# Retention and two MLPs on one core: where the first chunk's increments, weight conversions and warm-up matmuls stand

## The chip, the core and the metric

The kernel runs on one core of a Trainium2 chip. Its time is the device time of one execution in microseconds (us). The core has a matrix engine (PE, with its weight loads shown as PEld), a vector engine (DVE), a scalar engine (ACT), GpSimd (POOL) and SyncE (SP); the last two only issue DMAs here, SP the loads and POOL the stores. Each engine takes its instructions in the order in which they stand. PE writes its results to PSUM, from which DVE and ACT read them.

## What is computed

The reference runs a decaying linear attention ("retention") over 768 tokens for 4 batches and 8 heads of 64, and sends the result, as a matrix of 3072 tokens by 512, through two MLPs with 2048 hidden units.

```
state = gamma * state + k_t (x) v_t          # per batch and head, 64 x 64
y_t   = scale * q_t @ state
x = y reshaped to 3072 x 512
x = leaky(x @ w_in) @ w_out                  # leaky(h) = max(0.01 h, h)
out = relu(x @ w2_in)**2 @ w2_out
```

The weights come as 64-bit numbers whose words are float64 bit patterns; the kernel turns them into float32 itself, and then splits each float32 matrix into a high and a low part, so that a product is three matmuls (high by high, low by high, high by low).

## The kernel before

The tokens are worked in chunks of 256 (`C`), and a pair `(u, p)` is one batch's chunk for two heads (`p` of `NP` = 4). The first chunk has 16 pairs, numbered here 0 to 15 in the order of `ups`, and they are what the program does first, with the first weights being loaded and converted beside them. In the first chunk a pair's work is dealt over two turns of the start loop (`for n in range(n0 + 1)`):

- `scores(pair n)`: four score matmuls into the tile `sc` (two PSUM banks, tag `sc`, two buffers) and two matmuls of `increment`, the sum of k (x) v over the pair's first 128 tokens, into columns 256 to 319 of the first of these banks. DVE multiplies the scores by the decay mask (`pm`, line 220), and ACT copies the increment to SBUF (`s1`, line 235), which is the state after 128 tokens.
- `values(pair n-1)`: matmuls into a bank `y` of the pool `ps_h` (three banks, tag `h`): state times q, the second increment, masked scores times v. Then ACT casts y to `xh` (line 272), DVE makes the new `state` (line 278) and the low part `xl` (line 282), and the bank is free.
- `prep_pair` scales q (DVE, line 179) and v (ACT, line 189) for a pair that comes two turns later.

Between these stand the steps of `first_in(q)`, a generator that converts the input weights of hidden tiles 0 and 1 (`in_steps`): ACT scales the high words (`high`) and the low words (`low`), DVE shifts, puts in the sign and adds, and `up` splits the result into `wa`. One step is taken per turn from turn 6 on, two from turn 14. `emit_plain(q, i, t)` is a projection of 512 tokens by 128 hidden units: 12 matmuls into a bank `pa` of `ps_h`, then an Lrelu on ACT (line 741), then for t = 0 the split into `gh` (ACT, 762) and `gl` (DVE, 763). It stands after turn 14 for hidden tile 0, and for tile 1 after the loop.

`make_out(q)` converts the output weights of hidden tiles 2q and 2q+1: `cast` (ACT lines 382, 383; DVE lines 384, 385, 388) and then `pair_up` into `wo` (ACT line 414, DVE line 415). `put_out` (through `emit_out`) multiplies by `wo` into the banks `acc`; its first call comes after the projection `emit_plain(1, 0, 0)`.

The order on each engine is the order of emission where an instruction goes through `pin` (all matmuls and DMAs, and everything in `seq` while `strict[0]` is set). What is not pinned is placed by a scheduler. `aside()` holds it back: its instructions are issued after the two marked instructions (`mark`), which are here the last projection's Lrelu. `load_w(q, half)` puts the load of a raw weight tile `sg` (two buffers) on SP's queue; half 0 is the input part, half 1 the output part. A load waits in SP's queue until its buffer is free, and the loads behind it wait with it.

The start of the program makes `busy(WARM)` matmuls on zeros into the bank `idle`.

Of the kernel before, what the change touches and what calls it, by code (L numbers as in the profile page):

```python
# [9 lines left out]
F32 = mybir.dt.float32  # L10
# [3 lines left out]
AF = mybir.ActivationFunctionType  # L14
ALU = mybir.AluOpType

B, H, S, D = 4, 8, 768, 64
P = 128
C = 256
# [6 lines left out]
T = 512  # L26
# [3 lines left out]
NJ = DFF // P  # L30
NQ = NJ // 2
FW = 1024
WARM = 6

# [17 lines left out]
def retention_then_two_mlps(  # L54
# [9 lines left out]
    nc = tc.nc  # L64
# [7 lines left out]
    ps_h = ctx.enter_context(tc.tile_pool(name="ps_h", bufs=3, space=bass.MemoryType.PSUM))  # L72
# [30 lines left out]
    @contextmanager  # L103
    def aside():

        with tc.issue_after(mark[0]), tc.issue_after(mark[1]):
            yield
# [14 lines left out]
    def seq(ins):  # L122

        return pin(ins) if strict[0] else ins
# [9 lines left out]

    ups = [(b, p) for t in range(2) for p in range(NP) for b in (2 * t, 2 * t + 1)]
    ups += [(c * B + b, p) for c in range(1, NC) for p in range(NP) for b in range(B)]
    raw, prep, sc_ps, ps = {}, {}, {}, {}
    xs = {}


# [60 lines left out]
    def scores(up, alone):  # L201
        u, p = up
        c, b = divmod(u, B)
        raw_qk = raw[up][0]
        if u < B:
            sc2 = ps["s"].tile([P, 2, 512], F32, tag="sc", name="sc")
            sc = [sc2[:, h] for h in range(2)]
        else:
            other = (ps["a"], "y") if alone else (ps_h, "h")
            sc = [p.tile([P, 512], F32, tag=t, name="sc") for p, t in ((ps_h, "h"), other)]  # L210
        for s in range(2):
            t = slice(s * P, s * P + P)
            for h in range(2):
                a = slice(64 * h, 64 * h + 64)
                mm(out=sc[h][:, t], lhsT=raw_qk[a, C + t.start:C + t.stop], rhs=raw_qk[a, t], start=True, stop=True)
        sp = sc[0][:, C:C + D]
        increment(up, 0, sp)
        if u < B:
            both = prep[up][2]
            seq(nc.vector.tensor_tensor(  # L220
                out=both.rearrange("p h (s t) -> p h s t", t=P),
                in0=sc2[:, :, 0:C].rearrange("p h (s t) -> p h s t", t=P),
                in1=mk[p].unsqueeze(2).to_broadcast([P, 2, 2, P]), op=ALU.mult,
            ))
            pm = [both[:, h] for h in range(2)]
        else:
            pm = [a_p.tile([P, C], F32, tag="pm", name="pm") for h in range(2)]
            for h in range(2):
                nc.vector.tensor_tensor(
                    out=pm[h].rearrange("p (s t) -> p s t", t=P), in0=sc[h][:, 0:C].rearrange("p (s t) -> p s t", t=P),  # L230
                    in1=mk[p][:, h].unsqueeze(1).to_broadcast([P, 2, P]), op=ALU.mult,
                )
        s1 = a_p.tile([P, D], F32, tag="s1", name="s1", bufs=3)
        if c == 0:
            seq(nc.scalar.copy(s1, sp))
        else:
            nc.vector.scalar_tensor_tensor(
                out=s1, in0=state[:, b, p], scalar=gt[p], in1=sp, op0=ALU.mult, op1=ALU.add,
            )
        sc_ps[up] = pm, s1  # L240

    def values(up):
        u, p = up
        c, b = divmod(u, B)
        vk = raw[up][1]
        qs = prep[up][0]
        pm, s1 = sc_ps.pop(up)
        y = (ps["a"] if c else ps_h).tile([P, T], F32, tag="y" if c else "h", name="y")
        for s in range(0 if c else 1, 2):
            st = s1 if s else state[:, b, p]  # L250
            for h in range(2):
                a = slice(64 * h, 64 * h + 64)
                mm(
                    out=y[a, s * P:s * P + P], lhsT=st[a], rhs=qs[a, s],
                    start=s == 0 or not c, stop=False, skip_group_check=True,
                )
        if c < NC - 1:
            increment(up, 1, y[:, C:C + D], False)
        for s in range(2):
            for h in (1, 0):  # L260
                mm(
                    out=y[64 * h:64 * h + 64, s * P:s * P + P], lhsT=vk[:, s * P + h * D:s * P + h * D + D],
                    rhs=pm[h][:, s * P:s * P + P], start=False, stop=True, skip_group_check=True,
                )
        if c == 0:

            t, kh = b // 2, p // 2
            if (t, kh) not in xop:
                i = ((1, 5), (6, 3))[t][kh]
                xop[t, kh] = [x_p.tile([P, 2, T], F32R, tag=f"x{l}{i}", name=f"x{l}{i}") for l in "hl"]  # L270
            hi, lo = (x[:, p % 2, b % 2 * C:b % 2 * C + C] for x in xop[t, kh])
            seq(nc.scalar.copy(hi, y[:, 0:C]))
        else:
            if c not in xs:
                xs[c] = x_p.tile([P, KB, TB], F32, tag="xs", name="xs")
            nc.scalar.copy(xs[c][:, p, b * C:b * C + C], y[:, 0:C])
        if c < NC - 1:
            seq(nc.vector.scalar_tensor_tensor(
                out=state[:, b, p], in0=s1, scalar=gt[p], in1=y[:, C:C + D], op0=ALU.mult, op1=ALU.add,
            ))  # L280
        if c == 0:
            seq(nc.vector.tensor_tensor(out=lo, in0=y[:, 0:C], in1=hi.bitcast(F32), op=ALU.subtract))
        prep.pop(up)
        raw.pop(up)
# [53 lines left out]
    def load_w(q, half):  # L338
        if q == NQ:
            return  # L340
        t = stage[q, half] = w_p.tile([P, 1024], U64, tag="sg", name="sg", bufs=2)
        load(out=t, in_=w1[q, half])
# [74 lines left out]
    def in_steps(s, f, to):  # L417

        word = s.bitcast(U32).rearrange("p (n t) -> p n t", t=2)
        h = [slice(0, 512), slice(512, 1024)]  # L420
        lo, hi = word[:, :, 0], word[:, :, 1]
        ru = f.bitcast(U32)

        def high(c):
            seq(nc.scalar.activation(out=f[:, c], in_=hi.bitcast(F32)[:, c], func=AF.Copy, scale=2.0 ** -112))
            seq(nc.vector.tensor_scalar(
                out=ru[:, c], in0=ru[:, c], scalar1=3, scalar2=None, op0=ALU.logical_shift_left,
            ))

        def low(c):  # L430
            seq(nc.scalar.activation(out=lo[:, c], in_=lo[:, c], func=AF.Copy, scale=2.0 ** -29))

        def sign(c):
            seq(nc.vector.scalar_tensor_tensor(
                out=ru[:, c], in0=hi[:, c], scalar=0x80000000, in1=ru[:, c], op0=ALU.bitwise_and, op1=ALU.bitwise_or,
            ))

        def add(c):
            seq(nc.vector.tensor_tensor(out=ru[:, c], in0=ru[:, c], in1=lo[:, c], op=ALU.add))

        def up(n):
            t, r = to[:, :, 2 * n:2 * n + 2], f[:, h[n]].rearrange("p (n c) -> p n c", n=2)
            seq(nc.scalar.copy(t[:, 0], r))
            seq(nc.vector.tensor_tensor(out=t[:, 1], in0=r, in1=t[:, 0].bitcast(F32), op=ALU.subtract))

        high(h[0])
        yield
        low(h[0])
        sign(h[0])
        yield  # L450
        high(h[1])
        add(h[0])
        yield
        low(h[1])
        sign(h[1])
        yield
        add(h[1])
        yield
        up(0)
        yield  # L460
        up(1)
# [95 lines left out]
    def make_out(q):  # L557
        if q < NQ - 1:
            f = g_p.tile([P, 2, T], F32, tag=f"t{NQ - 1}", name="of", bufs=1).rearrange("p j c -> p (j c)")
        else:  # L560
            f = w_p.tile([P, 1024], F32, tag="wf", name="of", bufs=1)
        cast(stage.pop((q, 1)), f, 1 if q else 2)
        o = o_p.tile([P, 4, 2, 256], F32R, tag="wo", name="wo", bufs=2)
        pair_up(o.rearrange("p n l c -> p l n c"), f.rearrange("p (n c) -> p n c", n=4))
        put_wou(q, o)
# [430 lines left out]

    busy(WARM)
    n0 = B * NP
# [7 lines left out]
    for n in range(n0 + 1):  # L1006
        if n == 0:
            load_w(0, 0)
        loads_to(min(n + 6, n0))
        if n == 11:  # L1010
            loads_to(n0 + 2)
        if n in (6, 12):
            load_w(2 - n // 6, n // 12)
        score_next(n0)
        if n < 3:
            busy(2 - n // 2)
        if n in (6, 14):
            steps = first_in(n // 14)
        for _ in range(1 + (n > 13) if n < n0 else 0):
            next(steps, None)  # L1020
        value_to(min(n, n0))
        prep_to(min(n + (2 if n < 2 else 3), n0 + 2))
        if n == 14:
            emit_plain(0, 0, 0)
# [2 lines left out]
    load_w(1, 1)  # L1027
    emit_plain(0, 1, 0)
    strict[0] = False
    make_out(0)  # L1030
    start.close()
    ps["acc"] = ctx.enter_context(tc.tile_pool(name="ps_acc", bufs=1, space=bass.MemoryType.PSUM))
    ps["a"] = early.enter_context(tc.tile_pool(name="ps_a", bufs=1, space=bass.MemoryType.PSUM))
# [246 lines left out]
```

## Time and profile before

| | us |
|---|---|
| median of 3 runs | 1122.57 |
| lowest and highest of them | 1118.81, 1127.09 |
| profiled execution, its time | 1124.68 |
| profiled execution, its span | 1122.9 |

| engine | busy us | share of the span |
|---|---|---|
| PE | 1099.7 | 98% |
| DVE | 704.4 | 63% |
| ACT | 582.1 | 52% |

The span runs from the first to the last instruction of the profiled execution; its time holds 1.8 us around that. A busy share of an engine counts what the profile shows as running, at whatever clock. The chain of waits is the work that ended last, followed back from the end of the program.

### The profile page before, as it was taken

To read this page: it belongs to the slowest core of one execution; us is meant where nothing else is said; L and a number is where in the kernel's file an instruction comes from. 1 tells how busy PE (TensorE), PEld (TensorE's weight loads), DVE (VectorE), ACT (ScalarE), POOL (GpSimd) and SP (SyncE) were. 2 spreads that over 40 slices of the span, in tenths; PEclk is the share of its full clock that TensorE was granted. 3 is DMA by queue.
4 is the path that set the end of the run, shared out by engine and by line. 5 is a ranking of instruction groups with operands and counts; after the bars stand their busy time and mean duration, and the time that the engine had idled before them with its cause. 6 is when DMAs were issued, how large, how long until landed. Compare 5 with 4: busy or idle time off the path is not lost.

```text
span 1122.9 us, 15253 instructions
## 1 busy us (share of the span) xinstructions
PE 1099.7 (98%) x5643; PEld 872.4 (78%) x5643; DVE 704.4 (63%) x1205; ACT 582.1 (52%) x1052; POOL 78.0 (7%) x134
## 2 busy tenths in 40 slices
PE   9799999899999999999999999999999999999998
PEld 6477777678777776788788788788888888888886
DVE  4576766755657555526557738885745777555853
ACT  4466665534646453335555446655455555455542
POOL 0000100101000010001111021200100000000000
PEclk9899999999999999999999999999999999999999
DMA  9368887766598876588895877988245866357571
GB/s 366 131 240 312 326 285 233 280 198 228 208 351 299 335 264 222 190 313 322 327 316 197 321 275 271 354 325 317 112 169 197 327 206 262 112 191 249 180 243 57
DMA packets 81227, 283.87 MB, mean 253 GB/s; under 512 B 7808, under 2 KB 10368, under 8 KB 72960
## 3 DMA queue, kind: packets, MB, share of 16 engines
q1 hardware_dynamic: 64208, 210.33, 54.2%
q0 software_dynamic: 16800, 72.36, 16.5%
q8 instruction: 45, 0.74, 0.3%
q10 hardware_dynamic: 144, 0.20, 0.1%
q14 instruction: 30, 0.25, 0.1%
HBM read 205.79 MB, written 77.07 MB: 252 GB/s over the span
## 4 chain that ended last, share of the span: by engine, by line
PE 77%; issue 7%; DMA 7%; DVE 5%; ACT 2%; POOL 1%; SPq 0%; POOLq 0%; ACTq 0%; DVEq 0%
PE acc L127 38%; PE pa L127 21%; PE pd L127 7%; PE y L127 4%; PE pb L127 3%; DMA r<-first 3%; PE sc L127 3%; DMA sg<-w 2%; DMA wo<-wou 1%; POOL wou L133 1%; DMA of<-wflt 1%; PE idle L127 1%; DVE pm L220 0%; DMA wf<-wraw 0%; DVE of L385 0%
## 5 line engine op out<-in xcount | busy, mean ns | idle before, releaser
L127 PE MATMUL acc<-rot,wu 128*128 128x512 f32 x1008 | 235.7, 395 | 0.0
L127 PEld LDWEIGHTS acc<-rot,wu 128*128 128x128 f32 x1008 | 189.2, 188 | 46.0
L127 PE MATMUL pa<-xh,wa 128*128 128x512 f32 x576 | 181.2, 396 | 0.0
L127 PE MATMUL acc<-gh,wo 128*128 128x512 f32 x600 | 160.3, 399 | 3.4 <-DMA wo<-wou 2.5
L127 PEld LDWEIGHTS acc<-gh,wo 128*128 128x128 f32 x600 | 112.3, 189 | 31.6 <-issue 4.7
L127 PEld LDWEIGHTS pa<-xh,wa 128*128 128x128 f32 x576 | 106.3, 188 | 25.5 <-issue 2.2
L127 PE MATMUL pa<-xl,wa 128*128 128x512 f32 x288 | 112.6, 391 | 0.0
L837 ACT CAST rot<-gu 128x512 fp32r<-128x512 f32 x120 | 74.5, 621 | 61.5 <-PE acc L127 54.1
L838 DVE TENSOR_TENSOR rot<-gu,rot 128x512 fp32r<-128x512 f32 x120 | 82.1, 689 | 38.0 <-ACT rot L837 37.5
L127 PE MATMUL pa<-xh,wb 128*128 128x512 f32 x320 | 99.9, 393 | 0.8 <-DVE gt L863 0.8
L127 PE MATMUL pd<-xh,wa 128*128 128x512 f32 x320 | 99.1, 390 | 1.0 <-DVE wa L485 0.6
L127 PE MATMUL acc<-gl,wo 128*128 128x512 f32 x300 | 85.3, 391 | 0.0
L763 DVE TENSOR_TENSOR gl<-g,gh 128x512 fp32r<-128x512 f32 x75 | 50.6, 688 | 36.9 <-ACT gh L762 20.6
L127 PEld LDWEIGHTS pd<-xh,wa 128*128 128x128 f32 x320 | 60.0, 188 | 14.8 <-DVE wa L485 1.0
L127 PEld LDWEIGHTS pa<-xh,wb 128*128 128x128 f32 x320 | 59.4, 188 | 14.1 <-DVE gt L863 1.2
L127 PEld LDWEIGHTS acc<-gl,wo 128*128 128x128 f32 x300 | 56.5, 188 | 12.6
L127 PEld LDWEIGHTS pa<-xl,wa 128*128 128x128 f32 x288 | 54.1, 188 | 11.6
L127 PE MATMUL acc<-gg,wo 128*128 128x512 f32 x252 | 62.9, 398 | 0.0
L127 PE MATMUL pa<-xl,wb 128*128 128x512 f32 x160 | 62.4, 390 | 0.0
L127 PE MATMUL pd<-xl,wa 128*128 128x512 f32 x160 | 62.4, 390 | 0.0
L127 PEld LDWEIGHTS acc<-gg,wo 128*128 128x128 f32 x252 | 46.8, 188 | 11.9 <-issue 1.4
L687 ACT ACTIVATE gt<-gt 128x512 f32<-128x512 f32 x48 | 30.4, 633 | 48.4 <-DVE gt L856 34.3
(143 smaller groups left out, 1636.5 us busy)
## 6 DMA issues: line engine op xcount, KB each, us to landing
wu<-wou SPq DMA_DIRECT2D x84, 512.0 KB, 5.9
wo<-wou SPq DMA_DIRECT2D x32, 1024.0 KB, 7.9
wa<-wid SPq DMA_DIRECT2D x28, 1024.0 KB, 7.5
wb<-wid SPq DMA_DIRECT2D x28, 768.0 KB, 6.5
sg<-w SPq DMA_DIRECT2D x16, 1024.0 KB, 6.5
wou<-of POOLq DMA_DIRECT2D x32, 512.0 KB, 5.3
r<-first SPq DMA_DIRECT2D x50, 256.0 KB, 6.6
wid<-wa POOLq DMA_DIRECT2D x12, 1024.0 KB, 6.9
```

The costliest lines, as they stand in the source:

```text
L127: pin(nc.tensor.matmul(**kw))
L133: pin(nc.gpsimd.dma_start(**io))
L687: nc.scalar.activation(out=g, in_=g, func=AF.Relu)
L763: mark[1] = seq(nc.vector.tensor_tensor(out=gl, in0=g, in1=gh.bitcast(F32), op=ALU.subtract)).ins
L837: mark[0] = nc.scalar.copy(r[:, 0], s).ins
L838: mark[1] = nc.vector.tensor_tensor(out=r[:, 1], in0=s, in1=r[:, 0].bitcast(F32), op=ALU.subtract).ins
```

## The change

Four things, all in the start of the program:

- `WARM` goes from 6 to 10.
- In the first chunk the increment of the first 128 tokens goes into columns 320 to 383 of the pair's bank `y`, which is taken from its pool in `scores` and kept until `values`.
- The steps of `in_steps` are dealt anew: the shift stands apart from `high`, and a step holds one DVE operation. A conversion has eight steps where it had seven. `load_w(0, 1)`, the load of the first output weights, moves from turn 12 to turn 13.
- `make_out(0)` is in `aside()`.

```diff
-WARM = 6
+WARM = 10
...
-        sp = sc[0][:, C:C + D]
+        if u < B:
+            y = ps_y[up] = ps_h.tile([P, T], F32, tag="h", name="y")
+            sp = y[:, C + D:C + 2 * D]
+        else:
+            sp = sc[0][:, C:C + D]
         increment(up, 0, sp)
...
-        y = (ps["a"] if c else ps_h).tile([P, T], F32, tag="y" if c else "h", name="y")
+        y = ps["a"].tile([P, T], F32, tag="y", name="y") if c else ps_y.pop(up)
...
         def high(c):
             seq(nc.scalar.activation(out=f[:, c], in_=hi.bitcast(F32)[:, c], func=AF.Copy, scale=2.0 ** -112))
+
+        def low(c):
+            seq(nc.scalar.activation(out=lo[:, c], in_=lo[:, c], func=AF.Copy, scale=2.0 ** -29))
+
+        def shift(c):
             seq(nc.vector.tensor_scalar(
                 out=ru[:, c], in0=ru[:, c], scalar1=3, scalar2=None, op0=ALU.logical_shift_left,
             ))
-
-        def low(c):
-            seq(nc.scalar.activation(out=lo[:, c], in_=lo[:, c], func=AF.Copy, scale=2.0 ** -29))
...
-        high(h[0])
-        yield
-        low(h[0])
-        sign(h[0])
-        yield
-        high(h[1])
-        add(h[0])
-        yield
-        low(h[1])
-        sign(h[1])
-        yield
-        add(h[1])
-        yield
+        for ops in (
+            ((high, 0), (shift, 0)), ((low, 0), (sign, 0)), ((high, 1), (add, 0)), ((low, 1), (shift, 1)),
+            ((sign, 1),), ((add, 1),),
+        ):
+            for o, c in ops:
+                o(h[c])
+            yield
...
-        if n in (6, 12):
-            load_w(2 - n // 6, n // 12)
+        if n in (6, 13):
+            load_w(n % 2 == 0, n // 13)
...
-    make_out(0)
+    with aside():
+        make_out(0)
```

How this moves the instructions shows at three places. In the rows, a name ends in a number where the program numbered a tile, `[waits ...]` names the engines or DMA queues whose signal an instruction waits for, and the numbers of lines shift by a few between the two kernels.

ACT, turns 13 and 14 of the start loop, before (the copy of an increment, a split of `wa`, the low words of the first output weights, the cast of a y, the scaled v of a later pair):

```order
L235 COPY s_506<-sc 128x64 [waits DVE_49]
L443 CAST wa<-wf 128x512
L383 ACTIVATE sg<-sg 128x512 [waits DMAHW3_49,Activation_49]
L383 ACTIVATE sg<-sg 128x512
L272 CAST xh_452<-y 128x256 [waits PE_49]
L189 ACTIVATE pm<-r,tab_78 128x2x64 [waits DMAHW4_49]
L189 ACTIVATE pm<-r,tab_78 128x2x64
L235 COPY s_536<-sc 128x64 [waits DVE_49]
```

ACT at the same place in the changed kernel:

```order
L239 COPY s_511<-y 128x64 [waits DVE_49,PE_49]
L276 CAST xh_456<-y 128x256 [waits PE_49]
L189 ACTIVATE pm<-r,tab_78 128x2x64 [waits DMAHW4_49]
L189 ACTIVATE pm<-r,tab_78 128x2x64
L239 COPY s_538<-y 128x64 [waits DVE_49,PE_49]
L449 CAST wa<-wf 128x512
L276 CAST xh_456<-y 128x256 [waits PE_49]
```

The two operations on `sg`, which wait for a load, are gone from between the copy of one increment and the cast of the next y; the copy now reads the bank of y and waits for PE, where it waited for DVE.

ACT after the start loop, in the changed kernel: from the Lrelu of the projection of tile 1 (the first row) to the Lrelu after which `wo` is cast. Before, the operations of lines 386 and 387 (382 and 383 there) stood ahead of the first row, and the cast of `wo` (414) between the last two Lrelus:

```order
L741 ACTIVATE g<-pa 128x512 [waits PE_49]
L386 ACTIVATE of<-sg 128x512 [waits DMAHW3_49]
L387 ACTIVATE sg<-sg 128x512
L386 ACTIVATE of<-sg 128x512
L387 ACTIVATE sg<-sg 128x512
L762 CAST gh<-g 128x512 [waits Activation_49]
L741 ACTIVATE g<-pa 128x512 [waits PE_49] x2
L387 ACTIVATE sg<-sg 128x1024 [waits DMAHW4_49]
L418 CAST wo<-of 128x4x256 [waits DVE_49]
```

And the same stretch before:

```order
L741 ACTIVATE g<-pa 128x512 [waits PE_49]
L762 CAST gh<-g 128x512 [waits Activation_49]
L741 ACTIVATE g<-pa 128x512 [waits PE_49]
L414 CAST wo<-of 128x4x256 [waits DVE_49]
L741 ACTIVATE g<-pa 128x512 [waits PE_49]
L383 ACTIVATE sg<-sg 128x1024 [waits DMAHW4_49]
```

The cast of the first `wo` moved behind one more Lrelu and behind the first operation on the second output weights (128x1024), which waits for their load.

DVE, turns 8 and 9 of the start loop, before (mask, conversion of the input weights, state and low part of a finished pair, q of a later pair):

```order
L220 TENSOR_TENSOR pm<-sc,tab_78 128x2x256 [waits PE_49]
L426 TENSOR_SCALAR wf<-wf 128x512 [waits Activation_49]
L439 ISA wf<-sg,wf 128x1024 [waits DVE_49]
L278 SCALAR_TENSOR_TENSOR state<-s_378,tab_78,y 128x64 [waits Activation_49]
L282 TENSOR_TENSOR xl_326<-y,xh_325 128x256
L179 TENSOR_TENSOR pm<-r,tab_79 128x128 [waits DMAHW0_49]
```

and in the changed kernel:

```order
L224 TENSOR_TENSOR pm<-sc,tab_78 128x2x256 [waits PE_49]
L445 ISA wf<-sg,wf 128x1024 [waits DVE_49]
L282 SCALAR_TENSOR_TENSOR state<-s_384,tab_78,y 128x64 [waits Activation_49]
L286 TENSOR_TENSOR xl_331<-y,xh_330 128x256
L179 TENSOR_TENSOR pm<-r,tab_79 128x128 [waits DMAHW0_49]
```

The shift, which waits for ACT, left this turn; it stands one turn later.

## Rows read from the trace of the kernel before

**Rows 1.** Windows: us; busy PE, PEld, DVE, ACT, POOL; clock; DMA share; GB/s.

```profile
20.00:22.00 2.00, 2.00 (x32) 1.47 (x32) 1.42 (x4) 1.11 (x6) 0.00 (x0) 1.00 1.04 367
44.00:46.00 2.00, 1.38 (x10) 0.86 (x12) 1.20 (x4) 1.11 (x5) 0.00 (x0) 0.50 0.00 0
...
60.00:100.00 40.00, 40.00 (x226) 31.24 (x224) 27.17 (x41) 23.78 (x36) 3.25 (x5) 1.00 0.81 296
```

**Rows 2.** Timeline, turns 12 to 14: start us, us, engine, operation, [idle before <-releaser].

```profile
35.04 26.36 SPq L130 DMA_DIRECT2D sg<-w  x2
...
37.72 0.72 PE L127 MATMUL sc<-r 64*128 64x128 f32 x8
42.08 1.19 ACT L383 ACTIVATE sg<-sg 128x512 uint32<-128x512 uint32 x2 [4.97 <-DMA sg<-w]
...
43.88 0.77 PE L127 MATMUL sc<-pm,r 128*64 128x64 f32 x4 [5.45 <-ACT pm L189]
...
47.16 1.23 PE L127 MATMUL sc<-r 64*128 64x128 f32 x8
```

**Rows 3.** Timeline, turn 5, a turn without a conversion step.

```profile
19.61 0.71 PE L127 MATMUL sc<-r 64*128 64x128 f32 x8
...
20.87 0.68 DVE L220 TENSOR_TENSOR pm<-sc,tab 128x512 f32<-128x512 f32 x1
...
21.58 0.21 ACT L235 COPY s<-sc 128x64 f32<-128x64 f32 x1 [0.89 <-DVE pm L220]
21.59 0.71 PE L127 MATMUL sc<-r 64*128 64x128 f32 x8
```

**Rows 4.** Timeline, turns 7 to 11, with conversion steps.

```profile
24.91 0.42 DVE L282 TENSOR_TENSOR xl<-y,xh 128x256 fp32r<-128x256 f32 x1
...
26.19 0.34 PE L127 MATMUL sc<-pm,r 128*64 128x64 f32 x4
...
27.53 0.71 PE L127 MATMUL sc<-r 64*128 64x128 f32 x8
...
31.77 0.68 DVE L434 SCALAR_TENSOR_TENSOR wf<-sg,wf 128x512 uint32<-128x512 uint32 x1
...
32.15 0.44 PE L127 MATMUL y<-pm,s 64*64 64x128 f32 x4 [1.15 <-ACT s L235]
```

**Rows 5.** Timeline, the start of the program.

```profile
1.46 2.93 PE L127 MATMUL idle<-zero 128*128 128x512 f32 x6 [1.46 <-DVE zero L989]
...
4.41 0.93 PEld L127 LDWEIGHTS sc<-r 64*128 64x128 f32 x8 [0.74 <-DMA r<-first]
...
7.45 0.93 PEld L127 LDWEIGHTS sc<-r 64*128 64x128 f32 x8 [0.65 <-DMA r<-first]
...
15.16 0.52 PEld L127 LDWEIGHTS sc<-r 64*128 64x128 f32 x8 [0.17 <-issue]
```

**Rows 6.** Timeline, turn 15 and the end of the start loop.

```profile
53.87 0.72 PE L127 MATMUL sc<-r 64*128 64x128 f32 x8
...
56.85 0.44 PE L127 MATMUL y<-pm,s 64*64 64x128 f32 x4 [0.93 <-ACT s L235]
...
57.92 0.73 PE L127 MATMUL pa<-xh,wa 128*128 128x512 f32 x2
```

**Rows 7.** Timeline, the first output product and what it waits for.

```profile
65.93 1.05 ACT L414 CAST wo<-of 128x1024 fp32r<-128x1024 f32 x1 [1.62 <-DVE of L388]
...
67.01 1.23 DVE L415 TENSOR_TENSOR wo<-of,wo 128x1024 fp32r<-128x1024 f32 x1 [0.27 <-ACT wo L414]
...
67.57 0.60 ACT L741 ACTIVATE g<-pa 128x512 f32<-128x512 f32 x1 [0.59 <-PE pa L127]
...
68.06 1.13 ACT L383 ACTIVATE sg<-sg 128x1024 uint32<-128x1024 uint32 x1
...
68.75 0.73 PE L127 MATMUL pa<-xh,wa 128*128 128x512 f32 x2
...
71.60 0.63 PE L127 MATMUL acc<-gh,wo 128*128 128x512 f32 x2
```

More of the change, by code (lines that the diff above doesn't have):

```diff
@@ L136, in retention_then_two_mlps @@
     ups += [(c * B + b, p) for c in range(1, NC) for p in range(NP) for b in range(B)]
-    raw, prep, sc_ps, ps = {}, {}, {}, {}
+    raw, prep, sc_ps, ps_y, ps = {}, {}, {}, {}, {}
     xs = {}
```

## The prediction

> **What bounds the kernel now.** I read the windows first. From 60 us on PE is busy without a gap (40.00 of 40.00) at the full clock, so what the start of the program saves there should stay saved [rows 1]. The start itself is another matter, so the timeline of the first 75 us comes next.
>
> A turn of the start loop without a conversion step takes 1.98 us from one score group to the next (19.61 to 21.59), PE has no gap in it, DVE is busy 1.42 and ACT 1.11 of 2.00 [rows 1, 3]. That is the pace to compare everything with: PE bounds it. Four stretches are slower.
>
> The largest stands between turns 13 and 14: 9.44 us from score group to score group (37.72 to 47.16). ACT stands at line 383, the low words of the first output weights, 4.97 us for a load that SP could issue only at 35.04, because its buffer was still being read by the conversion of the first input weights. The cast of a y and the scaled v of the next pair stand behind it on ACT, and PE waits 5.45 us for that v [rows 2]. Nothing in the loop needs that output tile. After the gap PE runs at the low level: the window from 44 to 46 us shows 0.50 of the clock, which is 1.2 of 2.4 GHz, and a score group takes 1.23 instead of 0.71 [rows 1 to 3].
>
> **The change part by part.** The sum is made against the profiled execution: 1124.68 us, of which 1122.9 is the span. It lies 2.1 above the median of the three runs, 1122.57, and I take the saving over to the median unchanged.
>
> *Output tile behind the gate.* In the changed order the two operations of line 383 are gone from ACT's turn 13 and nothing else there waits for a load that late. Turn 13 then takes 1.98 instead of 9.44: **7.46 saved**. What follows on PE, turn 14 and the first projection, took 6.71 (47.16 to 53.87), most of it at the low clock [rows 2, 6]. At the full clock it is 1.98 and one projection, 2.85 by the one from 68.75 to 71.60 [rows 3, 7], so 4.83: **1.88 saved**, as PE has no pause left that could lower the clock.
>
> The price is that the conversion comes late. Its cast into `wo` now stands behind the Lrelu of the fourth projection (0.60) and the first operation on the second output tile (1.13); with cast and subtraction (1.05, 1.23) the chain is 4.01 from the start of that Lrelu, 4.1 to 4.3 with handoffs. The Lrelu began at 67.57 and the first output product at 71.60 [rows 7], 4.03 later, and its second matmul, 0.2 later still, is the first that reads the low half. So this costs 0 to 0.3; I take **0.2 lost**, where before `wo` was done at 68.24 (67.01 and 1.23), over 3 us ahead. The cover is gone, and any delay of ACT there is now PE's.
>
> *Conversion steps and the increment's bank.* Turns 9 to 12 took 10.19 us (27.53 to 37.72), four plain turns 7.92: 2.27 is lost to conversions [rows 2 to 4]. The lost time shows as PE waiting for the copy of the increment (1.15 at 32.15), and that copy begins when the mask ends (20.87 and 0.68, then 21.58), since both read one bank [rows 3, 4]. With the increment in y's bank the copy follows PE, and the mask no longer waits for the increment. What is left is DVE's own load: 1.42 and one operation of at most 0.68 to 0.69 is 2.10 per turn against 1.98 [rows 1, 4]. Six of the eight turns with a step carry such a long operation, so at most 0.7 in all would remain, and the first part of it hides in the slack between mask and use. The gain is 1.5 to 2.27; I take **2.0**, nearer to the upper end because PE uses a mask a turn after its scores.
>
> Holding a bank of y from `scores` on makes PE's increment of pair n wait until pair n-3 has left its bank. Before, with DVE in a conversion turn, the low part of pair 5 ended at 25.33 (24.91 and 0.42) and the increment of pair 8 ran at 26.19 [rows 4]: 0.86 to spare. I cost this at nothing; DVE hides it. If that cover goes, a turn waits for what DVE is late. The Trainium skill, "PSUM — Partial Sum Buffer", in its summary of rules for kernel authors, tells to evacuate PSUM promptly because it is tight, which speaks against taking a bank a turn early; by the row's 0.86 it costs nothing and the sum stands. By the rule, if DVE's one long operation (0.68) were missing in each of six turns, it would cost 4.1 and leave 9.7, an estimate.
>
> At the end of the loop 4.05 lies between the score group of pair 15 and the next projection, 0.93 of it PE waiting for the last increment's copy, which stood behind the mask [rows 6]. That wait goes, a shorter one for the mask itself stays: 0.3 to 0.93, I take **0.7 saved**. The changed program lets that projection take the bank of the projection before it, so it need not wait for pair 14.
>
> The load of the first output weights goes one turn later on SP, where the buffer's release (the last addition of the first conversion) moves a turn too. Nothing behind it on SP can run earlier than the release of the other buffer, as before. No POOL store changes its place.
>
> *Warm-up.* Six matmuls took 2.93 [rows 5], so four more are up to 4 x 0.49 = 1.95. Of this the first score group's wait for its data (0.74) and the second's (0.65) are covered anyway [rows 5], so the third pair comes at most 0.6 later: the one end. The other end: from 7.45 to 15.16, two turns, PE ran at the low level for most of the time (a group's weight loads take 0.93, at 15.16 they take 0.52) and took 7.71 [rows 5]. All at the full clock it is 7.71 x 0.71 / 1.23 = 4.45, 3.3 less; with the 0.6, 2.7 saved. What PE did before the clock rose: the two waits for data, then work without a pause as long. With ten matmuls both waits are filled, so I expect the rise soon after the first score group. I take **2.0 saved**, between 0.6 lost and 2.7 saved, since pauses for ACT's casts of a new y will cost some.
>
> In "TensorE: Matmul & The Clock Gate", part 1, on the clock gate, the Trainium skill says that the count of slow matmuls at the start varies from run to run, and should not be fitted. By that rule the start would count for nothing, and the sum be 11.8.
>
> *The sum:* 7.46 + 1.88 + 2.0 + 0.7 - 0.2 + 2.0 = **13.8 saved**. The profiled execution would have taken 1110.9; from the median it is **1108.8**, which I call 1109 (-1.2%).
>
> **The rivals.** *The start gives nothing:* the clock rises no sooner and the four matmuls only delay. 11.8 saved, or 11.2 with the 0.6: 1110.8 to 1111.4. For it: so few matmuls. Against it: both pauses ahead of the rise are filled.
>
> *The wait moves:* on ACT the first operation on the second output tile stands ahead of the cast of `wo` and needs its own load, which SP issues when the conversion of input tile 1 ends. SP's two issues ended at 61.40 (35.04 and 26.36) and ACT used the data at 68.06 [rows 2, 7], so a load takes at most 6.7. Walking the changed order with these durations, the last addition ends about 6.7 after the score group of pair 15 and ACT comes to that operation at 13.4: just in time. A load that is 5 us slower costs 5 and again about 2 at the low clock: 7 of 13.8 lost, 1115.6. For it: no slack. Against it: that transfer has the queue to itself.
>
> *The gain is given back:* from 60 to 100 us the DMA engines are busy 0.81 of the time [rows 1]. If transfers, not releases by PE, set the pace up to the first output products, PE would wait for weights and about half stays: 1115.6 to 1116. Against it: PE never waits there, and SP's issues wait for buffers that PE, ACT and DVE release, which all come earlier.
>
> *Slower:* the bank of y. If DVE's low part of pair n-3 came over 0.86 later against PE than in rows 4, each increment would wait, the scores behind it too, and DVE would set the pace. It decides for a loss from 13.8 / 13 = 1.1 us per turn, at 3.1 us a turn; at 3.3 the time is 1108.8 + 13 x 1.3 = 1125.7. Against it: DVE's load is 2.1 a turn, not 3.1.
>
> *It does not do what it says:* the ACT order shows that line 383 has left turn 13; only another wait of ACT there could undo it, and none for a load stands there.
>
> **How the numbers follow.** The forecast has 0.58, and 0.06 more for a better one (1105 to 1106, the upper ends of all terms); the start giving nothing 0.14, the moved wait 0.12, the gain given back 0.08, slower 0.02. One per cent, 11.2 us, is about what a measurement of this kernel can tell from no change; it lies at 1111.3. Faster by more: the first two and half of the third, 0.7. Within it: 0.28. Slower: 0.02. The range goes from 1105 to 1116, which takes in all but the worse parts of the moved wait and of the gain given back.
>
> **What would show it.** Line 387 (383 before) no longer between turns 12 and 14 on ACT, no pause of PE over 1.2 us from 8 to 60 us, turns of 1.98 to 2.1 throughout, and no window at 0.50 after the rise. The first output product should start at about 57 to 58 us instead of 71.60, with `wo` ready at nearly that time. The rise of the clock should come before the third score group. It is wrong if PE waits there for the load of the second output tile, if increments wait for DVE, or if new pauses of PE appear between 60 and 260 us.

## The result, and the profile after

The changed kernel takes 1108.32 us (median of 4 runs, 1107.05 to 1112.96) against 1121.57 for the kernel before (4 runs, 1118.81 to 1127.09): 13.2 us less, a ratio of 0.988 with a 95% interval of 0.984 to 0.993. The forecast was 1109 with 13.8 saved. The profiled execution took 1108.09, with a span of 1106.3.

The windows of the changed kernel come first (busy PE, PEld, DVE, ACT, POOL; clock; DMA share; GB/s), at the places of [rows 1].

```profile
20.00:22.00 2.00, 2.00 (x32) 1.47 (x32) 1.83 (x6) 1.92 (x7) 0.00 (x0) 1.00 1.03 410
44.00:46.00 2.00, 2.00 (x11) 1.62 (x9) 1.97 (x5) 0.14 (x1) 0.00 (x0) 1.00 0.00 0
60.00:100.00 40.00, 40.00 (x217) 31.47 (x217) 27.39 (x39) 23.66 (x36) 2.54 (x4) 1.00 0.85 306
```

PE is full in all three, and the window from 44 to 46, which was at 0.50, is at 1.00. The timeline of the changed kernel answers to [rows 2, 3, 4, 6]: one turn with a conversion step, the turn in which PE used to stand, and the end of the loop.

```profile
24.98 0.72 PE L127 MATMUL sc<-r 64*128 64x128 f32 x8
...
26.03 0.21 ACT L239 COPY s<-y 128x64 f32<-128x64 f32 x1
...
26.40 0.68 DVE L224 TENSOR_TENSOR pm<-sc,tab 128x512 f32<-128x512 f32 x1
...
32.90 0.72 PE L127 MATMUL sc<-r 64*128 64x128 f32 x8
...
34.88 0.72 PE L127 MATMUL sc<-r 64*128 64x128 f32 x8
...
39.81 0.71 PE L127 MATMUL sc<-r 64*128 64x128 f32 x8
...
43.13 0.72 PE L127 MATMUL pa<-xh,wa 128*128 128x512 f32 x2
```

The copy of the increment (26.03) runs ahead of the mask (26.40); before, it began when the mask ended [rows 3]. The first output product and the conversion that it needs, which answer to [rows 7]:

```profile
53.26 1.13 ACT L387 ACTIVATE sg<-sg 128x1024 uint32<-128x1024 uint32 x1
...
54.28 1.04 ACT L418 CAST wo<-of 128x1024 fp32r<-128x1024 f32 x1
...
55.36 1.23 DVE L419 TENSOR_TENSOR wo<-of,wo 128x1024 fp32r<-128x1024 f32 x1 [0.43 <-ACT wo L418]
...
56.80 0.63 PE L127 MATMUL acc<-gh,wo 128*128 128x512 f32 x2
```

`wo` is done at 56.59, 0.21 ahead of the product. The two profiled executions, leg by leg (each from one matmul group to another):

| leg | before | after | saved | predicted |
|---|---|---|---|---|
| to the fourth score group | 15.16 | 12.62 | 2.54 | 2.0 |
| fourth to tenth score group | 12.37 | 12.36 | 0.01 | 0 |
| turns 9 to 12 | 10.19 | 7.92 | 2.27 | 2.0 |
| turn 13 | 9.44 | 1.98 | 7.46 | 7.46 |
| turn 14 and the first projection | 6.71 | 4.93 | 1.78 | 1.88 |
| turn 15, end of the loop | 4.05 | 3.32 | 0.73 | 0.7 |
| from there to the first output product | 13.68 | 13.67 | 0.01 | -0.2 |
| the rest of the span | 1051.3 | 1049.5 | 1.8 | 0 |

The first line of the table says that the warm-up did what was forecast. The experiments say otherwise.

### The profile page after: what moved, and what is told of

The parts are those of the page before. It is cut to its first block, busy times and chain, and to the rows that moved or that the text cites. A ratio compares the mean times of both kernels' runs of the same rounds, so it can differ in the third digit from the quotient of the medians.

```text
span 1106.3 us, 15285 instructions
## 1 busy us (share of the span) xinstructions
PE 1094.2 (99%) x5647; PEld 869.0 (79%) x5647; DVE 703.6 (64%) x1205; ACT 582.0 (53%) x1052; POOL 77.6 (7%) x134
## 4 chain that ended last, share of the span: by engine, by line
PE 82%; issue 8%; DMA 5%; DVE 3%; POOL 1%; ACT 1%; SPq 0%; POOLq 0%; DVEq 0%; ACTq 0%
PE acc L127 38%; PE pa L127 23%; PE pd L127 8%; PE y L127 5%; PE pb L127 4%; PE sc L127 3%; DMA r<-first 3%; DMA wo<-wou 1%; DMA wflt<-sf 1%; POOL wou L133 1%; PE idle L127 1%; DMA wou<-of 0%; DMA wf<-wraw 0%; DVE gl L763 0%; DVE of L389 0%
## 5 line engine op out<-in xcount | busy, mean ns | idle before, releaser
L127 PEld LDWEIGHTS pd<-xh,wa 128*128 128x128 f32 x320 | 60.0, 188 | 15.2 <-DVE wa L485 1.4
```

The source lines that it names most:

```text
L127: pin(nc.tensor.matmul(**kw))
```

## The experiments

Two times are taken from every trace below: **A**, the start of the fourth score group, and **B**, from there to the first output product. B does not hold the start. In the kernels that have the bank and lack the pause it lies between 44.17 and 44.23; where the pause stands it varies more, by 0.77 between the two profiles of before.

| kernel | A | B | median, runs | ratio to before, 95% |
|---|---|---|---|---|
| before, the first profile | 15.16 | 56.44 | 1121.57, 4 | |
| before, a second profile | 12.81 | 57.21 | 1118.83, 1 | |
| bank alone | 12.80 | 52.88 | 1119.61, 10 | 0.998 (0.995 to 1.000) |
| gate alone | 12.74 | 49.69 | 1114.13, 4 | 0.993 (0.992 to 0.995) |
| gate and new steps | 12.98 | 47.80 | 1114.13, 4 | 0.993 (0.991 to 0.996) |
| bank and new steps | 13.14 | 44.19 | 1108.41, 4 | 0.989 (0.986 to 0.992) |
| bank and gate, old steps | 13.61 | 44.17 | 1108.70, 4 | 0.988 (0.983 to 0.992) |
| changed kernel, the first profile | 12.62 | 44.18 | 1108.32, 4 | 0.988 (0.984 to 0.993) |
| changed kernel, a second profile | 13.38 | 44.19 | 1108.87, 5 | 0.987 (0.984 to 0.989) |
| changed, 6 warm-up matmuls | 12.39 | 44.23 | 1108.01, 4 | 0.988 (0.986 to 0.990) |
| changed, 14 warm-up matmuls | 14.65 | 44.18 | 1109.83, 1 | |
| before, the pause filled | 12.62 | 54.84 | 1119.12, 10 | 0.997 (0.995 to 1.000) |
| changed, early pairs | 11.47 | 44.18 | 1107.62, 4 | 0.987 (0.981 to 0.992) |
| lean | 10.92 | 44.20 | 1108.16, 4 | 0.986 (0.984 to 0.989) |

The kernels with new steps and the one with bank, gate and old steps have ten warm-up matmuls, the bank and the gate alone have six. No kernel leaves out work of the reference. A ratio is to the runs of the kernel before that were made beside it, whose median was 1121.54 for the gate alone, the two kernels with new steps and a part missing, and the six warm-up matmuls; 1120.56 for the bank alone, the filled pause, the old steps and the early pairs; and 1123.23 for the lean kernel and the second profiles. Each A and B comes from one profile.

**The gate alone**, on the kernel before:

```diff
-    make_out(0)
+    with aside():
+        make_out(0)
```

> The kernel before, with one part of the change alone: the conversion of the first output tile stands behind the gate. Theory (an in-order wait of ACT): the pause between turns 13 and 14 goes (9.44 us to about 2.0) and with it the low clock after it, together 9.3 saved; the slow turns 9 to 12 (10.19), the end of the loop (4.05) and the third score group at 15.16 stay as they are. First output product at about 62.3 instead of 71.60, time about 9 below before. Rival (the conversion steps of the second input tile or DVE make the pause, not the wait): it stays at 7 us or more, time within 2 us of before. Rival (the gain is given back by loads before the gate): first output product later than 65.

The first output product came at 62.43, as expected, but not by the expected sum: the start was 2.42 earlier by itself (A), and B fell by 6.75 and not by 9.3. The waits of PE in the first 70 us of this kernel (total, times, longest) show where most of the rest is:

```profile
PE y L127 <- ACT s L235: 5.1, 7, 1.1
```

The wait for ACT's late v (5.45 in [rows 2]) is gone, but seven waits for the copy of an increment are left, where the kernel before had five with 3.6 in all. Turn 13 took 2.81 and not 1.98, turn 14 and the projection 5.75 and not 4.83: what the pause and the low clock had covered shows. The two rivals fall.

One part of B is not the gate's. In this profile turns 6 and 8 took 2.16 and 2.59 us where the kernel before took 1.98, 0.78 more up to the tenth score group. ACT had waited for a pair's load in turn 5, and PE then waited for a copy in turn 8:

```profile
19.02 0.69 ACT L189 ACTIVATE pm<-r,tab 128x128 f32<-128x128 f32 x2 [1.34 <-DMA r<-first]
...
24.82 0.44 PE L127 MATMUL y<-pm,s 64*64 64x128 f32 x4 [0.54 <-ACT s L235]
```

The kernel with the filled pause (below) has the same steps and the same bank, a wait of 0.54 for that load, and 1.98 in these turns. Without the 0.78 the gate alone is worth 7.53 of B; that the late load is the cause is read from these two profiles alone.

**Without the gate**, the changed kernel with `make_out(0)` outside `aside()`.

> The changed kernel without the gate part: the output tile is converted as soon as the program comes to it. In this program the two operations of the first output tile stand on ACT at turn 15, not in turn 13, since the load is asked for a turn later and the steps are one turn apart. Naive rival (the gate is the whole gain): the pause comes back in full, time 7 to 9 us above the changed kernel. Theory: the price is the landing of the load, about 38.5 us in the changed kernel, less the time at which ACT comes to the operation, about 36 to 37; so a pause of PE of 0 to 2 us, and if it is over 1 us some low clock behind it: time 0 to 3 us above the changed kernel, and the output weights ready several us ahead of the first output product.

B is 44.19, as with the gate, and the naive rival falls. In this program the two operations stand at turn 15, and the load has come by then; SP's issue, ACT's operation (no wait for DMA), and the end of the conversion, 3.91 ahead of the product at 57.33:

```profile
32.08 15.54 SPq L130 DMA_DIRECT2D sg<-w  x2
...
38.56 1.23 ACT L387 ACTIVATE sg<-sg 128x512 uint32<-128x512 uint32 x2
...
52.21 1.21 DVE L419 TENSOR_TENSOR wo<-of,wo 128x1024 fp32r<-128x1024 f32 x1
```

So in this profile the pause had two cures in the changed kernel, each enough: the gate, and the new place of the load and the steps (these two were not taken apart, nor tried without the bank). The second has little to spare. The load landed 5.9 us after its issue here, and in seven other profiles 6.1 to 8.6 after it; had it taken the 8.2 of the first profile of the changed kernel, ACT would have waited about 1.7 us for it (an estimate: 32.08 + 8.2 - 38.56). The four runs of this kernel lie 7.3 us apart (1104.12 to 1111.38), and only the fastest has a profile, so whether the pause came back in a slower one is open.

**Six warm-up matmuls** in the changed kernel (`WARM = 6`).

> The changed kernel with 6 matmuls in the warm-up, as before, instead of 10. Theory (four more matmuls bring the rise of the clock forward): the rise comes behind the third score group again, which starts the fourth group at about 15.2 us instead of 12.62; time 2.5 us above the changed kernel. Rival (the start's gain comes from the increments in the bank of y or varies by itself): the fourth score group at 12.6 to 13.2, time within 1 us of the changed kernel.

The fourth score group came at 12.39, not at 15.2, and the time is 1108.01. The theory falls: with six matmuls the slow ones ended ahead of the second score group.

```profile
4.41 1.22 PE L127 MATMUL sc<-r 64*128 64x128 f32 x8
...
6.85 0.71 PE L127 MATMUL sc<-r 64*128 64x128 f32 x8
```

**The increment back in the bank of the scores**, in the changed kernel:

```diff
-            y = ps_y[up] = ps_h.tile([P, T], F32, tag="h", name="y")
-            sp = y[:, C + D:C + 2 * D]
+            sp = sc[0][:, C:C + D]
...
-        y = ps["a"].tile([P, T], F32, tag="y", name="y") if c else ps_y.pop(up)
+        y = (ps["a"] if c else ps_h).tile([P, T], F32, tag="y" if c else "h", name="y")
```

> The changed kernel with the increment back in the bank of the scores. Theory (the mask holds that bank, and the copy of the increment waits for it): turns 9 to 12 take 9.5 to 10.2 us again instead of 7.92 and the end of the loop 4.0 instead of 3.32; PE shows waits for the copy of about 1.15 us; time 2 to 3 us above the changed kernel. Rival (splitting the conversion into one DVE operation per step did it): turns 9 to 12 stay at 7.9 to 8.3, time within 0.7 us of the changed kernel.

Turns 9 to 12 took 9.51, the end of the loop 4.51, and turn 14 grew as well (2.79): B is 3.62 longer, more than expected, and the median 5.8 longer. One such turn (the mask, the copy behind it, PE's wait for the copy):

```profile
25.80 0.68 DVE L223 TENSOR_TENSOR pm<-sc,tab 128x512 f32<-128x512 f32 x1
...
26.51 0.21 ACT L238 COPY s<-sc 128x64 f32<-128x64 f32 x1 [0.89 <-DVE pm L223]
...
26.77 0.44 PE L127 MATMUL y<-pm,s 64*64 64x128 f32 x4 [0.45 <-ACT s L238]
```

**The old steps** in the changed kernel, with the load in turn 12 again (the hunk on the steps, taken back as well, is not printed here):

```diff
-        if n in (6, 13):
-            load_w(n % 2 == 0, n // 13)
+        if n in (6, 12):
+            load_w(2 - n // 6, n // 12)
```

> The changed kernel with the seven old conversion steps and with the load of the first output weights asked for in turn 12 again; gate, bank of y and ten warm-up matmuls stay. Theory (the bank is what freed the turns; with it the copy no longer stands behind the mask): turns 9 to 12 at 7.9 to 8.4 us, first output product at 56.8 to 57.5, time within 1 us of the changed kernel. Rival (one DVE operation per step is needed as well, since two of 0.68 and 1.42 of other work are 2.8 in a turn of 1.98): turns with two operations at 2.3 to 2.8, turns 9 to 12 at 9 or more, first output product later by 1.5 to 2.5, time 1.5 to 2.5 above.

Turns 4 to 14 took 1.98 each, four of them 7.92 (turns 9 to 12), B is 44.17: with the bank of y one DVE operation per step is worth nothing.

```profile
25.98 0.71 PE L127 MATMUL sc<-r 64*128 64x128 f32 x8
...
33.90 0.71 PE L127 MATMUL sc<-r 64*128 64x128 f32 x8
```

Without the bank B is 1.89 shorter with the new steps (49.69 against 47.80); 0.78 of that is the late load of the gate-alone profile, and the times don't show the rest (both medians are 1114.13).

**The bank alone**: of the change only the hunks on `ps_y` and `sp`.

> The kernel before with the increments in the bank of y and nothing else: old steps, no gate, six warm-up matmuls. The output tile's two operations stand in turn 13 on ACT as in the kernel before. Theory: turns 9 to 12 fall to 7.9 to 8.4 us, the pause between turns 13 and 14 stays (turn 13 at 8 to 11 us, since the load is released with the conversion and takes as long as before) with the low clock behind it, and the end of the loop falls by 0.7; time 2.5 to 4 below the kernel before, 9 to 11 above the changed kernel. Rival (the pause came from the late turns): turn 13 below 5, time within 3 of the changed kernel.

Turns 9 to 12 took 7.93, the end of the loop 3.33, and the pause stayed, 0.53 longer than before (turn 13 took 9.97):

```profile
38.52 1.19 ACT L387 ACTIVATE sg<-sg 128x512 uint32<-128x512 uint32 x2 [7.61 <-DMA sg<-w]
...
40.77 0.48 PE L127 MATMUL y<-pm,r 128*64 128x64 f32 x4 [6.97 <-ACT s L239]
```

ACT waits 7.61 instead of 4.97 [rows 2]. Of these 2.64 us, 1.18 come from ACT, which is there sooner after the load's issue (0.89 us instead of 2.07), so the pause eats a part of what the bank saves; the other 1.46 come from the load, which took longer (issued at 30.02, used at 38.52: 8.50, where it was 35.04 to 42.08: 7.04). B fell by 3.56. The measured times fell by less (0.998), though the interval takes 3.56 in.

**The pause filled**, on the kernel before, behind the score group of pair 13:

```diff
         sp = sc[0][:, C:C + D]
+        if up == ups[13]:
+            busy(22)
```

> The kernel before with 22 idle matmuls (4.7 to 5 us at the full clock) in the pause of turn 13, so that PE waits for ACT as long but is not idle. Theory (the pause is what lowers the clock, and the low clock costs what the first experiment leaves for it): turn 13 still about 9.4 to 9.6, no window at 0.50 after it, score group of pair 14 at 0.71 instead of 1.23, turn 14 and the first projection 5.75 (as with the gate alone) instead of 6.71; so 0.9 to 1 saved. Prediction's term: 1.88 saved, 4.83. Rival (the low clock has another cause): window at 0.50 again. The start is that of the kernel before, six warm-up matmuls: a third look at when the matmuls get fast there.

The idle matmuls took 5.28, PE still waited for ACT behind them, and the clock did not fall; the idle matmuls with the wait behind them, the window of this kernel (PE, clock, DMA share, GB/s) and the next score group:

```profile
35.84 5.28 PE L127 MATMUL idle<-zero 128*128 128x512 f32 x22
41.51 0.62 PE L127 MATMUL sc<-pm,r 128*64 128x64 f32 x4 [0.39 <-ACT pm L189]
```

```profile
44.00:46.00 2.00, 1.23 (x18) 1.00 0.00 0
```

```profile
43.97 0.71 PE L127 MATMUL sc<-r 64*128 64x128 f32 x8
```

Turn 14 and the projection took 5.78 instead of 6.71, 0.93 less, and the end of turn 13, from the increment to the next score group, 2.46 instead of 3.28 [rows 2]. In the kernel before, the clock had fallen while PE stood (columns as in [rows 1]):

```profile
40.00:42.00 2.00, 0.00 (x0) 0.00 (x0) 0.00 (x0) 0.00 (x0) 0.00 (x0) 0.76 0.74 299
42.00:44.00 2.00, 0.12 (x1) 0.12 (x2) 0.44 (x2) 1.92 (x5) 0.00 (x0) 0.50 0.02 6
```

So the idle PE is what lowered the clock there. B fell by 1.60 against the first profile of before, and by 2.37 against the second.

**The start again**: the kernel before, the changed kernel, and 14 warm-up matmuls.

> The kernel before, unchanged: a second look at its start. If the six warm-up matmuls are why the score groups stayed slow to the third, the fourth score group starts at 15.2 us again. If the time of the rise varies by itself, as the four other looks at six matmuls say, it starts at 12.4 to 12.9.

> The changed kernel, unchanged, on the same chip as the lean one: fourth score group at 12.6 to 13.6 us, 44.18 from there to the first output product, time 1108 to 1109.

> The changed kernel with 14 warm-up matmuls. Prediction's term (matmuls ahead of the first scores bring the rise forward): no slow matmul behind them and a fourth score group no later than 12.6 us. Rival (the rise comes when it comes, the matmuls only stand ahead of the first scores): four more at 0.22 to 0.49 are 0.9 to 2.0, fourth score group at 13.5 to 14.6; 44.18 from there to the first output product.

In its second profile the kernel before had the fourth score group at 12.81, with the second one already at 0.71 (first three rows). Its pause was shorter (4.63 instead of 5.45), but the low clock behind it lasted longer: turn 14 and the projection took 8.30 (44.01 to 52.31, last two rows) instead of 6.71.

```profile
1.45 2.93 PE L127 MATMUL idle<-zero 128*128 128x512 f32 x6 [1.45 <-DVE zero L989]
4.31 1.23 PE L127 MATMUL sc<-r 64*128 64x128 f32 x8
...
7.27 0.71 PE L127 MATMUL sc<-r 64*128 64x128 f32 x8
...
44.01 1.23 PE L127 MATMUL sc<-r 64*128 64x128 f32 x8
...
52.31 0.71 PE L127 MATMUL sc<-r 64*128 64x128 f32 x8
```

With 14 the matmuls end at 7.6 and the fourth score group starts at 14.65, 1.3 to 2.0 later than in the two profiles of the changed kernel with ten:

```profile
1.46 6.15 PE L127 MATMUL idle<-zero 128*128 128x512 f32 x14 [1.46 <-DVE zero L989]
7.54 0.72 PE L127 MATMUL sc<-r 64*128 64x128 f32 x8
```

Over all kernels with the idle matmuls behind the first pairs, A is 15.16, 12.74, 12.39, 12.80, 12.62 and 12.81 with six warm-up matmuls (mean 13.09) and 12.62, 13.14, 12.98, 13.61 and 13.38 with ten (mean 13.15). Only the first profile of before has the long slow start; without it the mean with six is 12.67. One slow start in six profiles and none in five are too few to say whether ten matmuls guard against it.

**Early pairs**, on the changed kernel (with `WARM = 8`), and **lean**, which is the kernel before with bank, gate and early pairs, six warm-up matmuls and the old steps:

```diff
-        if n == 0:
-            load_w(0, 0)
         loads_to(min(n + 6, n0))
+        if n == 2:
+            load_w(0, 0)
...
-        if n < 3:
-            busy(2 - n // 2)
```

> The changed kernel with 8 warm-up matmuls, no idle matmuls behind the first three pairs and the first input weights asked for after the eighth pair. Those five idle matmuls take 1.96 us in the changed kernel. Theory (they stand on PE's path there, since PE has no pause in turns 0 to 3): first output product 0.5 to 2 us earlier, with pauses for the data of the pairs as the limit. Rival (turns 0 to 3 are bound by the data or by the casts of a y, and the idle matmuls only fill): no gain, pauses of 0.3 to 0.7 in their place, the slow matmuls of the start lasting longer, time 0 to 3 above the changed kernel.

> The kernel before with three things alone: the increments in the bank of y, the gate for the first output tile, and no idle matmuls behind the first three pairs (the first input weights asked for after the eighth pair). Six warm-up matmuls and the old conversion steps stay. Theory (bank and gate are the whole gain, the warm-up and the new steps add nothing): 44.18 us from the fourth score group to the first output product as in the changed kernel, fourth score group at 11 to 12 us, so first output product at 55.2 to 56.2, time 0.5 to 1.5 below the changed kernel. Rival (ten warm-up matmuls are needed once the idle ones are gone): fourth score group at 13 or later with matmuls at 1.23 until then, time 1 or more above.

Both came out as their theories had it in the trace: the idle matmuls stood on PE's path. From the first to the fourth score group PE took 6.30 in early pairs and 6.60 in lean, where the other profiles took 7.11 to 8.50 (the first of before 10.75). The first output product starts at 55.65 and 55.12, against 56.80 and 57.57 in the two profiles of the changed kernel. In the time it cannot be told: 1107.62 and 1108.16, the latter beside 1108.87 for the changed kernel on the same chip, with runs that overlap. The lean kernel shows, by its B of 44.20, that bank and gate are enough for the whole gain behind the start, without new steps and more warm-up.

## Why the prediction came out right, and where it was wrong

*The stall.* Right in the profile of the change (7.46), and the cause is shown: with the gate alone the wait for v is gone, with the bank alone it stays and follows the load. But the two parts share the term. The gate alone brings turn 13 down to 2.81, 6.63 saved; the last 0.83 came with the bank, and with the new steps as well (turn 13 is 1.98 with gate and new steps too).

*The low clock after it.* Sized 1.88 in turn 14 and the projection, 1.78 there in the changed kernel. The filled pause shows that the clock made 0.93 of that; the other 0.85 was waits for the copy of an increment, the bank's again (turn 14 and the projection still take 5.75 with the gate alone). The prediction took all above a plain turn for slow clock; it missed the slow matmuls at the end of turn 13, which it counted as stall. Nor is the term a constant: by the second profile of before it is 3.37 (8.30 less 4.93).

*The bank and the steps.* The mechanism of the bank is shown by the increment's copy in both directions; 2.27 came where 2.0 was taken, the upper bound. The steps, which the prediction joined with the bank, add nothing beside it. The bank held longer costs nothing: no wait of PE for it in the changed kernel. That is against the estimate of 4.1 which the prediction set beside the rule on prompt evacuation of the Trainium skill ("PSUM — Partial Sum Buffer", summary of rules for kernel authors); its condition (an operation of DVE missing in each of six turns) does not arise, as turns 4 to 14 are 1.98 each.

*The late `wo`.* 0.2 lost was predicted, 0.01 saved came. From the Lrelu to the end of `wo` it took 3.82 (52.77 to 56.59) and not 4.1 to 4.3: the prediction added handoffs, where each of the two operations of ACT behind the Lrelu began about 0.1 before the one ahead of it had ended. `wo` is ready 0.21 ahead of its use. Without the gate it was ready 3.91 ahead.

```profile
52.77 0.60 ACT L741 ACTIVATE g<-pa 128x512 f32<-128x512 f32 x1 [2.24 <-PE pa L127]
```

*The end of the loop.* 0.73 for 0.7.

*The warm-up is the step that failed:* "With ten matmuls both waits are filled, so I expect the rise soon after the first score group. I take 2.0 saved". The matmuls did get fast there, and 2.54 was saved in the profiles, but with six matmuls they got fast as early, and so they did for before in its second profile. No saving by the four matmuls shows (means of A 13.09 and 13.15), and four more on top cost 1.3 to 2.0 in their one profile. The error was to take one slow start for a property of the kernel. The Trainium skill says in "TensorE: Matmul & The Clock Gate", part 1, that the number of slow matmuls at the start varies from run to run and should not be fitted; these traces agree (with six warm-up matmuls the score groups were slow to the third in one profile, and the first alone in five).

*The sum.* Without the warm-up the prediction's terms are 11.8; B fell by 12.26 against the first profile of before and by 13.02 against the second, whose B was longer. With A on equal means that is 12.2 to 13.0 against measured 13.2 (14.4 in the second comparison, where before took 1123.23). That the forecast of 13.8 was so near is in part luck: 2.0 that no other profile shows stood beside terms that were 0.4 to 1.2 too small. By the experiments the first rival's mechanism (the start gives nothing) is the one that came, though not its time. What is left, 0.2 to 2.2 us, is inside the intervals and was not followed; the rest of the span runs from 1045.0 to 1052.1 over the 14 profiles, in no order of the kernels.

*How the parts add up.* In B the bank alone saves 3.56 and the gate alone 6.75, together 12.27: 1.96 more than the sum. Of this 0.78 is the late load in the profile of the gate alone, and against the second profile of before, whose pause and low clock were others, the surplus without that load is 0.4. So the parts do not simply add, but by how much is not settled. Turn 13 shows where: the bank alone makes it 0.53 longer, the gate alone 6.63 shorter, both together 7.46 shorter, since the pause takes up a part of what the turns before it gain, and waits for ACT's copies take up a part of what the pause leaves.

## What to carry to other kernels

Look for the operation that waits for a load in order in front of work that the bottleneck needs soon: moving the operation behind that work took the pause away here, and so did, in one profile, changing when its load is asked for and when the engine comes to it, though that hung on how long the load took. What such an operation costs is the pause and the slow matmuls behind it. Parts that cure one wait share its price, so that each has to be taken away alone and with the others. Where two engines read different results out of one bank and one waits for the other, try the smaller result in another bank. And before counting a slow start as a term, look at more than one profile of it: repeat the kernel before, or change something far behind the start.

## What the runs showed of the hardware

The granted clock in the profile does not show the slow start. In the first profile of before the window from 12 to 14 us stands at 1.00, though the score group at 12.05 took 1.23 as the one at 47.16 did, at 0.50; the durations have to be read there. The window:

```profile
12.00:14.00 2.00, 2.00 (x15) 1.00 1.07 435
```

Late in the program PE waits 1.6 to 3.4 us for the load of a `wo`, in all profiles, and in some of them the clock falls to 0.50 (1.2 of 2.4 GHz) behind it. In the first profile of the changed kernel the wait is 2.5 us:

```profile
606.00:608.00 2.00, 0.68 (x4) 1.00 1.03 406
608.00:610.00 2.00, 0.80 (x2) 0.75 1.04 416
610.00:612.00 2.00, 2.00 (x6) 0.50 1.03 406
```

With bank, gate and old steps the wait is 1.8 us, and the clock stays:

```profile
606.00:608.00 2.00, 1.66 (x8) 1.00 1.02 405
608.00:610.00 2.00, 0.57 (x3) 1.00 1.03 413
610.00:612.00 2.00, 2.00 (x10) 1.00 1.04 413
```

It stayed after a wait of 2.9 in the kernel with the gate alone, and fell after one of 2.0 in the one with 14 warm-up matmuls. The two profiles of the kernel before differ in it as well (it fell in the first and stayed in the second), so it is a part of the spread between runs of one kernel; how large a part was not measured.
